# Score products of a fused attention and expert kernel: all in fp32 without split operands, half-chunk loads, two score banks, expert weights in buffers of their own

## The chip, the cores and the metric

The kernel runs on one core of a Trainium2 chip. The metric is the device time of one execution in microseconds (us). The engines are named as the profile names them: PE (TensorE, matrix products; PEld is its weight load), DVE (VectorE), ACT (ScalarE), POOL (GpSimd), SP (SyncE, which here only issues loads). All data are fp32 in memory. The inputs are random.

## The reference

The program has two halves, one feeding the other. With B = 4, N = 5056, C = 256:

```python
qn = q / (norm(q, axis=1) + 1e-6); kn = k / (norm(k, axis=1) + 1e-6)
a  = softmax(kn.transpose(0, 2, 1) @ qn / tau)      # [B, 256, 256]
x  = (v @ a).reshape(20224, 256)
skip = x @ w_skip > 0                               # only these rows go on
e  = argmax(x @ w_gate); g = 1 / sum(exp(logits - max))
x[skip] += g * (relu(x @ w1[e]) @ w2[e])            # 8 experts, 256 -> 1024 -> 256
```

So the scores are a sum over all 5056 tokens of a batch, the norms too (sums of squares over the tokens), and a batch's softmax can begin only when all of its tokens have been added. After it each token's row of `v` is multiplied by a 256 x 256 matrix, its expert is looked up, and the rows of one expert are gathered and put through two products.

## The kernel before

**Chunks.** The tokens are padded to 16 chunks (4 of each batch) of 1280 = 128 x 10. A chunk of q and of k is a tile of [128, 10, 256], which holds 10 slices j of 128 tokens each. Three kinds of work share PE:

- A: scores of a chunk, 10 steps of one slice (`scores`, lines 667-683). A step is two products, one for each half of the 256 rows of the score matrix, added up in PSUM.
- B: `v @ a` of a chunk, 5 steps of two slices (`attend`, lines 746-761), each of 12 products of fp32r halves. The matrix `a` and `v` are split into a rounded part H and a rest L (H@H + L@H + H@L).
- H: the first 7 tiles of 512 rows of the expert half, done ahead (`first_ahead`, `second_ahead`) among the last chunks of B: four steps of the first product and two of the second. They work on the tokens of the first 8 chunks.

After these come the loop over full tiles of the expert half (`Large.loop`) and one over small tiles (`Small.loop`).

**How a score step is computed.** Of the 10 slices of a chunk, slices 3 to 9 go to PE in plain fp32 (line 682, which the profile shows as two passes a product). Slices 0 to 2 are split first: ACT copies q and k to fp32r (line 622), POOL or DVE subtracts that from the original (line 625), and PE multiplies `ks_H` by the pair (`qs_H`, `qs_L`), 512 columns (line 679), and `ks_L` by `qs_H`, 256 columns (line 680). In a chunk the plain slices come first. The sums stand in two PSUM banks, one for each half of the rows, with one buffer for both (`ps_s`, bufs=1). The softmax of a batch begins by copying both to SBUF and adding their two column halves (lines 689 and 694).

**Other work on q and k.** ACT squares each half chunk (line 646), DVE adds the squares up (line 650) and folds them at the end of a batch (lines 655-657), and PE adds over partitions (lines 662-664, the tile `n`).

**Loads.** q and k are loaded by SP into three buffers of a chunk each (1280 KB apiece; the first four chunks in parts), `v` into three buffers of a half chunk. POOL writes each routed token's number and gate into the lists of the experts by 10 indirect scatters a chunk (line 839), and it gathers and scatters the rows of the expert half.

**Expert weights.** `w1r` and `w2r` hold the raw weights of the expert whose rows are done ahead. They lie in a pool that is opened where the A tiles were, so that their gathers (line 223) come after the last A step. They are split by ACT and DVE (lines 311 and 313).

**Order.** A planner (`Plan`) sets the order of all of this at build time. Each task has an engine, a cost in us, the tasks that it waits for and, for PE, a nominal time that comes from the string `ORDER`; the planner runs a list schedule with these costs and emits the instructions engine by engine in that order. On the chip each engine then takes its instructions strictly in that order, and waits where one isn't ready. So wrong costs don't make a wrong result, but an order in which an engine waits for something late while other work stands ready behind it.

Of the kernel before, what the change touches and what calls it, by code (L numbers as in the profile page):

```python
# [145 lines left out]
def attn_moe(ctx: ExitStack, tc: tile.TileContext, q, k, vt, tau, w_skip, w_gate, w1, w2, out):  # L146
# [430 lines left out]
    ps_s = in_a.enter_context(tc.tile_pool(name="ps_s", bufs=1, space=PSUM))  # L577
# [21 lines left out]
    qk, spl, vs, sums, norms, augs, lg, xos, pxs = {}, {}, {}, {}, {}, {}, {}, {}, {}  # L599
# [4 lines left out]
    def load_qk(c, j0, j1):  # L604
        b, ch = divmod(c, NCH)
        if c not in qk:
            qk[c] = [pa.tile([P, J, C], F32, name=n, bufs=3) for n in ("qt", "kt")]
        js = slice(j0, j1)
        for t, src in zip(qk[c], (q, k)):
            nc.sync.dma_start(t[:, js, :], src[b, ch * P * J : (ch + 1) * P * J, :].rearrange("(p j) c -> p j c", j=J)[:, js, :])  # L610
# [6 lines left out]

    def split_qk(c, n, part, engine=None):
        t = qk[c][n][:, :JS, :]
        if part == 0:  # L620
            spl.setdefault(c, [None, None])[n] = pa.tile([P, JS, 2, C], F32R, name=("qs", "ks")[n], bufs=1)
            S.copy(spl[c][n][:, :, 0, :], t)  # L622
        else:
            s = spl[c][n]
            {"V": V, "G": G}[engine].tensor_tensor(s[:, :, 1, :], t, s[:, :, 0, :], ALU.subtract)  # L625
# [13 lines left out]
    def squares(c, n, h):  # L639

        hs = slice(h * JH, (h + 1) * JH)
# [4 lines left out]
        S.activation(to, qk[c][n][:, hs, :], AF.Square)  # L646
# [19 lines left out]
    def scores(c):  # L666

        b, ch = divmod(c, NCH)
        if ch == 0:
            sums[b] = ps_s.tile([P, 2, 512], F32, name="s")  # L670
        qt, kt = qk[c]
        for n, j in enumerate([*range(JS, J), *range(JS)]):
            first, last = ch == 0 and n == 0, ch == NCH - 1 and n == J - 1
            for cb in range(2):
                o = sums[b][:, cb, :]
                cs = slice(cb * P, (cb + 1) * P)
                if j < JS:
                    qs, ks = spl[c]
                    T.matmul(o, ks[:, j, 0, cs], qs[:, j, :, :], start=first, stop=False, skip_group_check=True)
                    T.matmul(o[:, :C], ks[:, j, 1, cs], qs[:, j, 0, :], start=False, stop=last, skip_group_check=True)  # L680
                else:
                    T.matmul(o[:, :C], kt[:, j, cs], qt[:, j, :], start=first, stop=last, skip_group_check=True)  # L682
            yield

    def softmax(b):


        u2 = pb.tile([P, 2, 512], F32, name="u2")
        S.copy(u2, sums[b])
        u = u2[:, :, :C]  # L690
# [3 lines left out]
        V.tensor_tensor(u, u, u2[:, :, C:], ALU.add)  # L694
# [11 lines left out]
        a = u2[:, :, C:]  # L706
# [210 lines left out]
    for seg in ORDER.split():  # L917
# [19 lines left out]
    for c in range(NC):  # L937
        b, ch = divmod(c, NCH)
        ld = {}
        users = []  # L940
        for j0, j1 in PARTS.get(c, [(0, J)]):
            t = then("qk", add("D", 0.73 * (j1 - j0), lambda c=c, j0=j0, j1=j1: load_qk(c, j0, j1), due=1e9 if c else -99, hold=("part", 99) if ld else ("qk", 3)))
            t.users = [] if ld else users
            ld.update((j, t) for j in range(j0, j1))
        sp = [None, None]
        for n in range(2):
            sq = []
            for h in range(2):
                begins = ch == 0 and h == 0
                s0 = then(("sq", n), add("S", 1.18, lambda c=c, n=n, h=h: squares(c, n, h), [ld[j] for j in range(h * JH, (h + 1) * JH)], hold=None if begins else ("sqh", 3)))  # L950
                sq.append(s0)
# [9 lines left out]
            s0 = then(("sp", n), add("S", 0.75, lambda c=c, n=n: split_qk(c, n, 0), [ld[JS - 1], last_a]))  # L961
            t = sp[n] = add(*(("VG", (0.88, 1.8)) if n else ("G", 1.8)), None, [s0])
            t.f = lambda c=c, n=n, t=t: split_qk(c, n, 1, t.engine)
            users += [s0, t, *sq]
        g = scores(c)
        for j in range(J):
            deps = [ld[(j + JS) % J]] + (sp if j >= J - JS else [])
# [4 lines left out]
        users.append(t)  # L972
        if ch == NCH - 1:
            g = softmax(b)
            s0, = chain(g, ("S", 0.9), deps=[t])
            n0, = chain(g, ("T", 0.8), deps=[s0, summed[0], summed[1]])
            s = chain(g, ("V", 0.97), ("S", 1.65), ("V", 2.1), ("V", 1.45), ("S", 2.35), ("V", 0.75), deps=[n0])
# [232 lines left out]
```

## Time and profile before

| | |
|---|---|
| time, median of 3 runs | 863.21 us (861.93 to 866.31) |
| profiled execution | 867.48 us, span 864.8 us, mean granted clock of PE 0.968 |
| PE busy | 797.2 us, 92% of the span |
| DVE, ACT, POOL busy | 561.9 (65%), 394.0 (46%), 488.4 us (56%) |
| A steps on PE | from 6.3 to 251.8 us |
| B steps | from 71.9 to 439.7 us |
| first H step | at 275.68 us |
| loop over full tiles | first product at 496.6 us, last at about 775 us |
| HBM traffic | 115.98 MB read, 32.59 MB written |

The table's times of the stages are the first and the last start in PE's timeline. A row of the waits view names who waited, for whom, and then the total in us, the number of waits and the longest. In a row of windows the figures are the window, its length, the busy us (and instructions) of each engine in the order PE, PEld, DVE, ACT, POOL, the granted clock of PE as a share of full speed, the DMA engines' busy share and GB/s. In a timeline the figures are the start and the duration in us; what stands in brackets is the idle time of the engine before it and what ended it. PE's durations are modelled for their ends, so that the time of a step on PE is taken here from start to start.

### The profile page before, as it was taken

What the parts mean: (1) busy time and instruction counts of PE and PEld (TensorE: products, weight loads), DVE (VectorE), ACT (ScalarE), POOL (GpSimd) and SP (SyncE); (2) the same over time, 40 slices, a digit from 0 to 9 for tenths busy, and PEclk for the clock granted to TensorE, in tenths of its full rate; (3) what the DMA queues carried; (4) which work ended last, traced back from release to release, by engine and by line L of the source; (5) the groups of instructions that cost most, each with busy time, mean ns of one, the idle gap of its engine ahead of it and who ended that gap; (6) DMA issues with size and microseconds to landing.
All of it is one profiled execution on the core that took longest, in us unless ns stands there. A gap on an engine that the chain in (4) does not pass through costs nothing. (4 is left out here: it accounts for less than half of the span.)

```text
span 864.8 us, 13631 instructions
## 1 busy us (share of the span) xinstructions
PE 797.2 (92%) x4506; PEld 700.0 (81%) x4506; DVE 561.9 (65%) x1071; ACT 394.0 (46%) x615; POOL 488.4 (56%) x490
## 2 busy tenths in 40 slices
PE   6998999789885999999998799999999999998977
PEld 5887988678775899888887688888888888877876
DVE  3979788699985864563556755556564646556464
ACT  5769568477664443432331233333342424235444
POOL 5235378788875777567527563434334343436666
PEclk9999899898997999999999999999999999999999
DMA  8978678885527451521230241111111111106670
GB/s 319 419 280 307 238 281 261 299 320 195 184 88 267 138 164 39 184 92 38 92 83 26 73 169 49 43 49 49 49 43 48 37 48 44 49 12 240 225 296 10
DMA packets 55483, 126.36 MB, mean 146 GB/s; under 512 B 17269, under 2 KB 37517, under 8 KB 49809
## 3 DMA queue, kind: packets, MB, share of 16 engines
q1 hardware_dynamic: 14688, 62.99, 20.0%
q0 software_dynamic: 19520, 42.12, 14.7%
q10 hardware_dynamic: 21232, 20.72, 7.4%
q8 instruction: 22, 0.36, 0.2%
q14 instruction: 21, 0.16, 0.1%
HBM read 115.98 MB, written 32.59 MB: 172 GB/s over the span
## 5 line engine op out<-in xcount | busy, mean ns | idle before, releaser
L839 POOL DMA_INDIRECT lst<-pay,r_posi x160 | 184.2, 1151 | 80.5 <-issue 43.3
L216 POOL DMA_INDIRECT out<-xg,lc x78 | 80.6, 1034 | 129.8 <-DVE xg L347 113.0
L340 PE MATMUL po<-w2s,hH 128*128 128x512 f32 x384 | 136.4, 398 | 0.3 <-issue 0.3
L323 ACT ACTIVATE hH<-ph 128x512 fp32r<-128x512 f32 x96 | 57.5, 599 | 126.4 <-PE ph L320 126.4
L682 PE MATMUL s<-qt,kt 128*128 128x256 f32 x448 | 106.7, 386 | 7.9 <-DMA kt<-in_k 6.8
L341 PE MATMUL po<-w2s,hL 128*128 128x256 f32 x384 | 107.2, 279 | 0.0
L324 DVE SCALAR_TENSOR_TENSOR hL<-ph,hH 128x512 fp32r<-128x512 f32 x96 | 66.4, 692 | 54.7 <-ACT hH L323 53.3
L757 PE MATMUL px<-aH,vH 128*128 128x266 f32 x320 | 99.6, 311 | 1.3 <-ACT xo L764 1.3
L211 POOL DMA_INDIRECT xg<-out,lc x80 | 82.1, 1026 | 29.3 <-issue 18.0
L682 PEld LDWEIGHTS s<-qt,kt 128*128 128x128 f32 x448 | 83.0, 192 | 18.9 <-DMA qt<-in_q 6.3
L758 PE MATMUL px<-aL,vH 128*128 128x266 f32 x320 | 94.0, 294 | 0.0
L759 PE MATMUL px<-aH,vL 128*128 128x266 f32 x320 | 93.5, 292 | 0.0
L340 PEld LDWEIGHTS po<-w2s,hH 128*128 128x128 f32 x384 | 72.1, 188 | 17.2 <-issue 0.7
L764 ACT COPY xo<-px 128x532 f32<-128x532 f32 x80 | 47.7, 602 | 68.3 <-PE px L759 68.2
L340 PE MATMUL px<-w2s,hH 128*128 128x512 f32 x224 | 78.3, 393 | 0.0
L318 PE MATMUL ph<-xH,w1H 128*128 128x512 f32 x192 | 75.9, 395 | 2.0 <-DVE xL L288 2.0
L625 POOL TENSOR_TENSOR qs<-qt,qs 128x768 fp32r<-128x768 f32 x16 | 44.8, 2801 | 57.3 <-ACT qs L622 57.1
L319 PE MATMUL ph<-xL,w1H 128*128 128x512 f32 x192 | 75.6, 394 | 0.0
L320 PE MATMUL ph<-xH,w1L 128*128 128x512 f32 x192 | 75.6, 394 | 0.0
L341 PEld LDWEIGHTS po<-w2s,hL 128*128 128x128 f32 x384 | 72.3, 188 | 0.4
L286 ACT CAST xH<-pt 128x512 fp32r<-128x512 f32 x40 | 22.4, 591 | 101.0 <-PE pt L284 101.0
L757 PEld LDWEIGHTS px<-aH,vH 128*128 128x128 f32 x320 | 62.7, 196 | 3.3 <-ACT xo L764 2.0
(216 smaller groups left out, 1860.0 us busy)
## 6 DMA issues: line engine op xcount, KB each, us to landing
vf<-in_vt SPq DMA_DIRECT2D x32, 640.0 KB, 5.2
qt<-in_q SPq DMA_DIRECT2D x12, 1280.0 KB, 7.2
kt<-in_k SPq DMA_DIRECT2D x12, 1280.0 KB, 9.9
out<-xo ACTq DMA_DIRECT2D x12, 1280.0 KB, 9.1
qt<-in_q SPq DMA_DIRECT2D x7, 384.0 KB, 8.5
kt<-in_k SPq DMA_DIRECT2D x7, 384.0 KB, 8.3
lst<-pay,r_posi POOLq DMA_INDIRECT x160, 3.2
out<-xo ACTq DMA_DIRECT2D x4, 640.0 KB, 9.6
```

The source lines that it names most:

```text
L211: apart(G.indirect_dma_start(out=to, out_offset=None, in_=out[0:n, :], in_offset=IndirectOffsetOnAxis(ap=ls[:, 0:1], axis=0), bounds_check ...
L216: i = (G.indirect_dma_start(out=out, out_offset=IndirectOffsetOnAxis(ap=ls[:, 0:1], axis=0), in_=src, in_offset=None, bounds_check=NTOK - ...
L318: T.matmul(ph, self.w1H[:, fs], self.xH[:, kb, :], start=(kb == 0), stop=False)
L319: T.matmul(ph, self.w1H[:, fs], self.xL[:, kb, :], start=False, stop=False)
L320: T.matmul(ph, self.w1L[:, fs], self.xH[:, kb, :], start=False, stop=(kb == 1))
L340: T.matmul(po, self.hH[:, f, ts], self.w2s[:, f, :, :], start=(f == 0), stop=False, skip_group_check=True)
L341: T.matmul(po[:, :C], self.hL[:, f, ts], self.w2s[:, f, 0, :], start=False, stop=(f == NFB - 1), skip_group_check=True)
L682: T.matmul(o[:, :C], kt[:, j, cs], qt[:, j, :], start=first, stop=last, skip_group_check=True)
L757: T.matmul(px[:, i, :NA], vH[:, kb, js], aH[:, kb, :], start=(kb == 0), stop=False)
L758: T.matmul(px[:, i, :NA], vH[:, kb, js], aL[:, kb, :], start=False, stop=False)
L759: T.matmul(px[:, i, :NA], vL[:, kb, js], aH[:, kb, :], start=False, stop=(kb == 1))
L839: i = G.indirect_dma_start(out=lst, out_offset=IndirectOffsetOnAxis(ap=posi[:, t : t + 1], axis=0), in_=pay[:, t0 + t, :], in_offset=None, ...
```

## The change

It does these things together:

- All 10 slices of a chunk go to PE in plain fp32. The splits of q and k on ACT, POOL and DVE and the tiles `qs` and `ks` are gone.
- The sums of a batch take one bank (2 x 256 columns) instead of two, and there are two of them, so that a batch's first step waits for the softmax copy of the batch before the last one.
- The addition of the two column halves in the softmax is gone; the exponentials get a tile of their own.
- q and k are loaded by half chunks (640 KB each) into five buffers of a half chunk, where there were three of a whole one. A buffer is free when the squares of that half and its fifth step are done. The first half of chunk 0 is loaded in two parts.
- `w1r` and `w2r` get buffers of their own. Their gathers then wait only for the choice of the expert (`look`), and stand in POOL's order behind the scatters of chunk 7. The splits of the weights still go to tiles where A's tiles were, and so wait for the last A step.
- The costs that the planner uses are changed: a step of A 0.865 (0.86 and 0.65 before), of B 1.475 (1.34), of H 2.74 and 5.62 (2.56 and 5.15), a pair of scatters 2.6 (2.09) and some smaller ones, so that the order on every engine is another one. `ORDER` itself is the same.

```diff
-JS = 3
-
-PARTS = {0: [(3, 5), (5, J), (0, 3)], 1: [(3, 6), (6, J), (0, 3)], 2: [(3, 6), (6, J), (0, 3)], 3: [(3, 6), (6, J), (0, 3)]}
+NQ = 5
...
             self.xg = [rows([P, 4, C], F32, name=f"xg{h}") for h in range(3)]
+            self.w1r = rows([P, 2 * F], F32, name="w1r")
+            self.w2r = rows([P, NFB * C], F32, name="w2r")
...
         def weights(self):
             wp = ctx.enter_context(tc.tile_pool(name="wl", bufs=1, reuse_waits="tile"))
-            self.w1r = wp.tile([P, 2 * F], F32, name="w1r")
-            self.w2r = wp.tile([P, NFB * C], F32, name="w2r")
...
-    ps_s = in_a.enter_context(tc.tile_pool(name="ps_s", bufs=1, space=PSUM))
+    ps_s = in_a.enter_context(tc.tile_pool(name="ps_s", bufs=2, space=PSUM))
...
-    def load_qk(c, j0, j1):
+    def load_qk(c, h, j0, j1):
         b, ch = divmod(c, NCH)
-        if c not in qk:
-            qk[c] = [pa.tile([P, J, C], F32, name=n, bufs=3) for n in ("qt", "kt")]
+        if (c, h) not in qk:
+            qk[c, h] = [pa.tile([P, JH, C], F32, name=n, bufs=NQ) for n in ("qt", "kt")]
...
-    def split_qk(c, n, part, engine=None):
-        t = qk[c][n][:, :JS, :]
-        if part == 0:
-            spl.setdefault(c, [None, None])[n] = pa.tile([P, JS, 2, C], F32R, name=("qs", "ks")[n], bufs=1)
-            S.copy(spl[c][n][:, :, 0, :], t)
-        else:
-            s = spl[c][n]
-            {"V": V, "G": G}[engine].tensor_tensor(s[:, :, 1, :], t, s[:, :, 0, :], ALU.subtract)
...
-            sums[b] = ps_s.tile([P, 2, 512], F32, name="s")
-        qt, kt = qk[c]
-        for n, j in enumerate([*range(JS, J), *range(JS)]):
-            first, last = ch == 0 and n == 0, ch == NCH - 1 and n == J - 1
+            sums[b] = ps_s.tile([P, 2, C], F32, name="s")
+        for j in range(J):
+            qt, kt = qk[c, j // JH]
             for cb in range(2):
...
-                if j < JS:
-                    qs, ks = spl[c]
-                    T.matmul(o, ks[:, j, 0, cs], qs[:, j, :, :], start=first, stop=False, skip_group_check=True)
-                    T.matmul(o[:, :C], ks[:, j, 1, cs], qs[:, j, 0, :], start=False, stop=last, skip_group_check=True)
-                else:
-                    T.matmul(o[:, :C], kt[:, j, cs], qt[:, j, :], start=first, stop=last, skip_group_check=True)
+                T.matmul(sums[b][:, cb, :], kt[:, j % JH, cb * P : (cb + 1) * P], qt[:, j % JH, :], start=(ch == 0 and j == 0 and cb == 0), stop=(ch == NCH - 1 and j == J - 1), skip_group_check=True)
...
-        V.tensor_tensor(u, u, u2[:, :, C:], ALU.add)
...
-                    now += (0.88 if i < J - JS else 0.66) if x == "A" else 1.36 if x == "B" else 2.6 if i < 4 else 5.2
+                    now += 0.87 if x == "A" else 1.48 if x == "B" else 2.75 if i < 4 else 5.65
...
-            if j == 0 and ch == 0 and b:
-                deps.append(freed_s[b - 1])
-            t = then("A", add("T", 0.86 if j < J - JS else 0.65, lambda g=g: next(g), deps, nominal["A", c, j]))
+            if j == 0 and ch == 0 and b > 1:
+                deps.append(freed_s[b - 2])
+            t = then("A", add("T", 0.865, lambda g=g: next(g), deps, nominal["A", c, j]))
...
-            t = then("B", add("T", 1.34, None, [sv[j > 2][1], sv[j >= 2][1], ready_a[b]], nominal["B", d, j], hold=("px", 2, 1)))
+            t = then("B", add("T", 1.475, None, [sv[j > 2][1], sv[j >= 2][1], ready_a[b]], nominal["B", d, j], hold=("px", 2, 1)))
...
-        in_order["sc"] = chain(g, *[("G", 2.09)] * (J // 2), deps=[routed[d], in_order.get("sc")], due=nominal["B", d, 4] + 15)[-1]
+        in_order["sc"] = chain(g, *[("G", 2.6)] * (J // 2), deps=[routed[d], in_order.get("sc")], due=nominal["B", d, 4] + 15)[-1]
...
-    wg1 = add("G", 1.05, scores_done, [look, norms_read, last_a])
-    wg2 = add("G", 1.05, lambda: gather_w(w2, large.w2r, large.wd), [wg1])
-    wd1 = add("D", 2.9, None, [wg1])
-    wd2 = add("D", 2.9, None, [wg2])
+    wr1 = add("G", 1.3, lambda: gather_w(w1, large.w1r, large.wc), [look])
+    wr2 = add("G", 1.3, lambda: gather_w(w2, large.w2r, large.wd), [wr1])
+    wd1 = add("D", 2.9, None, [wr1])
+    wd2 = add("D", 2.9, None, [wr2])
+    wg1 = wg2 = add("S", 0.05, scores_done, [wr2, norms_read, last_a])
```

The sequence of the scheduled instructions shows what this moves. The first place is PE's first steps. Before:

```order
L682 MATMUL s<-qt,kt 128x256 x14
L679 MATMUL s<-qs,ks 128x512
L680 MATMUL s<-qs,ks 128x256
L679 MATMUL s<-qs,ks 128x512
L680 MATMUL s<-qs,ks 128x256
```

Now:

```order
L662 MATMUL s<-qt,kt 128x256 x110
L649 MATMUL n<-sqq,ones 128x256
L651 MATMUL n<-ones,sqk 128x2 x2
L662 MATMUL s<-qt,kt 128x256 x26
L703 MATMUL m<-ident,aug 128x128 x4
```

The products that read `qs` and `ks` are gone, and with them the places at which PE waits for the splits; the norms of batch 0 stand behind 55 steps, where they stood behind 53.

The second place is POOL between the last scatters of chunk 7 (`lst<-pay`) and the first gathers of rows (`xg<-out`), for which `lN` holds the list. Before:

```order
L228 TENSOR_LOAD ad_2347
L228 ISA x2
L229 ISA
L229 DMA lN<-lst 128x56
L625 TENSOR_TENSOR ks<-kt,ks 128x3x256
L389 COPY lc_151<-lN 128x8
L211 DMA xg_145<-out,lc_151 128x256 x4
L389 COPY lc_149<-lN 128x8
L211 DMA xg_143<-out,lc_149 128x256 x4
L223 DMA w1r<-in_w,wc 128x2048
L223 DMA w2r<-in_w,wd 128x2048
```

Now:

```order
L817 DMA lst<-pay,r_posi 168960x2 x80
L221 DMA w1r<-in_w,wc 128x2048
L221 DMA w2r<-in_w,wd 128x2048
L226 TENSOR_LOAD ad_2113
L226 ISA x2
L227 ISA
L227 DMA lN<-lst 128x56
L387 COPY lc_153<-lN 128x8
L209 DMA xg_145<-out,lc_153 128x256 x4
```

The 11 splits that stood among these scatters and behind them are gone (one of them, of `ks`, is among the rows of before), and the two gathers of raw weights have moved from behind eight gathers of rows to ahead of the list.

The third place is PE near the end of the work ahead: the count of chunk 15's tokens (`m<-r_rc`), on which the last scatters and all later lists wait. Before it stood between the two products of the sixth tile:

```order
L320 MATMUL px<-xH,w1L 128x512
L814 MATMUL m<-r_rc,tri_r 128x8
L815 MATMUL m<-r_rc,ones_r 128x8
L284 MATMUL pt<-ident,xg_145 128x128 x4
L340 MATMUL px<-w2s,hH 128x512
```

Now it stands in the middle of that tile's second product, one of its two steps later:

```order
L339 MATMUL px<-w2s,hL 128x256
L792 MATMUL m<-r_rc,tri_r 128x8
L793 MATMUL m<-r_rc,ones_r 128x8
L338 MATMUL px<-w2s,hH 128x512
```

More of the change, by code (lines that the diff above doesn't have):

```diff
@@ L597, in end_lists @@
         yield
-    qk, spl, vs, sums, norms, augs, lg, xos, pxs = {}, {}, {}, {}, {}, {}, {}, {}, {}
+    qk, vs, sums, norms, augs, lg, xos, pxs = ({} for _ in range(8))
     sqs = [pa.tile([P, JH, C], F32, name=f"sq{n}", bufs=1) for n in "qk"]
     sqh = {}
-    def load_qk(c, j0, j1):
+    def load_qk(c, h, j0, j1):
         b, ch = divmod(c, NCH)
-        if c not in qk:
-            qk[c] = [pa.tile([P, J, C], F32, name=n, bufs=3) for n in ("qt", "kt")]
-        js = slice(j0, j1)
-        for t, src in zip(qk[c], (q, k)):
-            nc.sync.dma_start(t[:, js, :], src[b, ch * P * J : (ch + 1) * P * J, :].rearrange("(p j) c -> p j c", j=J)[:, js, :])
+        if (c, h) not in qk:
+            qk[c, h] = [pa.tile([P, JH, C], F32, name=n, bufs=NQ) for n in ("qt", "kt")]
+        for t, src in zip(qk[c, h], (q, k)):
+            nc.sync.dma_start(t[:, j0:j1, :], src[b, ch * P * J : (ch + 1) * P * J, :].rearrange("(p j) c -> p j c", j=J)[:, h * JH + j0 : h * JH + j1, :])
     def load_v(n):
@@ L639, in squares @@
     def squares(c, n, h):
-        hs = slice(h * JH, (h + 1) * JH)
         if c % NCH == 0 and h == 0:
@@ L705, in softmax @@
         yield
-        a = u2[:, :, C:]
+        a = pb.tile([P, 2, C], F32, name="a")
         mx = pb.tile([P, 2], F32, name="mx")
@@ L938, in attn_moe @@
         b, ch = divmod(c, NCH)
[L939 to L945, printed above, removed]
+        ld, users = {}, ([], [])
+        for h in range(2):
+            for j0, j1 in [(0, 2), (2, JH)] if c == 0 and h == 0 else [(0, JH)]:
+                t = then("qk", add("D", 0.76 * (j1 - j0), lambda c=c, h=h, j0=j0, j1=j1: load_qk(c, h, j0, j1), due=1e9 if c else -99, hold=("part", 99) if j0 else ("qk", NQ)))
+                t.users = [] if j0 else users[h]
+                ld.update((h * JH + j, t) for j in range(j0, j1))
         for n in range(2):
-            sq = []
             for h in range(2):
@@ L960, in attn_moe @@
                 summed[n] = add("V", 1.53, lambda n=n: fold_squares(n), [summed[n]])
[L961 to L964, printed above, removed]
         g = scores(c)
         for j in range(J):
-            deps = [ld[(j + JS) % J]] + (sp if j >= J - JS else [])
-            if j == 0 and ch == 0 and b:
-                deps.append(freed_s[b - 1])
-            t = then("A", add("T", 0.86 if j < J - JS else 0.65, lambda g=g: next(g), deps, nominal["A", c, j]))
+            deps = [ld[j]]
+            if j == 0 and ch == 0 and b > 1:
+                deps.append(freed_s[b - 2])
+            t = then("A", add("T", 0.865, lambda g=g: next(g), deps, nominal["A", c, j]))
+            if j % JH == JH - 1:
+                users[j // JH].append(t)
         last_a = t
-        users.append(t)
         if ch == NCH - 1:
             g = softmax(b)
-            s0, = chain(g, ("S", 0.9), deps=[t])
+            s0, = chain(g, ("S", 0.5), deps=[t])
             n0, = chain(g, ("T", 0.8), deps=[s0, summed[0], summed[1]])
-            s = chain(g, ("V", 0.97), ("S", 1.65), ("V", 2.1), ("V", 1.45), ("S", 2.35), ("V", 0.75), deps=[n0])
+            s = chain(g, ("V", 0.42), ("S", 1.65), ("V", 2.2), ("V", 1.85), ("S", 2.35), ("V", 0.75), deps=[n0])
             m0, = chain(g, ("T", 0.45), deps=s[-1:])
@@ L1000, in attn_moe @@
         for h in range(2):
-            ld = then("v", add("D", 1.85, lambda d=d, h=h: load_v(2 * d + h), hold=("vf", 3)))
+            ld = then("v", add("D", 1.88, lambda d=d, h=h: load_v(2 * d + h), hold=("vf", 3)))
             s0 = then("vH", add("S", 1.18, lambda d=d, h=h: split_v(d, h, 0), [ld], hold=("vH", 3)))
@@ L1089, in attn_moe @@
             g = large.first_ahead(2 * i)
-            t = then("H", add("T", 2.56, None, tr + w1s[1::2], nominal["H", x, i], hold=("px", 2, 1)))
+            t = then("H", add("T", 2.74, None, tr + w1s[1::2], nominal["H", x, i], hold=("px", 2, 1)))
             t.f = lambda g=g, t=t: product(g, t)
@@ L1099, in attn_moe @@
             g = large.second_ahead(x, 2 * i)
-            t = then("H", add("T", 5.15, None, [v for n in range(4) for v in in_order["hL", n]] + w2s[1::2], nominal["H", x, 4 + i], hold=("px", 2, 1)))
+            t = then("H", add("T", 5.62, None, [v for n in range(4) for v in in_order["hL", n]] + w2s[1::2], nominal["H", x, 4 + i], hold=("px", 2, 1)))
             t.f = lambda g=g, t=t: product(g, t)
```

14 lines of the change are left out of this document (5 added, 9 removed).

## The prediction

> **What bounds the kernel now.** I read the windows by stage first: A alone to 66 us, A and B to 276, then B and H. Later instructions are the same in both kernels.
>
> ```profile
> core 0: us, PE busy (x) PEld busy (x) DVE busy (x) ACT busy (x) POOL busy (x), PEclk, DMA share, GB/s
> 0.00:66.00 66.00, 58.14 (x274) 49.98 (x274) 46.61 (x47) 42.52 (x45) 24.16 (x43) 1.00 0.87 340
> 66.00:100.00 34.00, 30.13 (x170) 26.82 (x170) 28.40 (x40) 26.28 (x31) 13.84 (x2) 0.90 0.77 287
> 100.00:276.00 176.00, 148.29 (x910) 135.75 (x909) 146.43 (x263) 113.36 (x152) 139.63 (x109) 0.92 0.68 236
> 276.00:494.00 218.00, 210.07 (x1201) 184.29 (x1201) 132.96 (x348) 75.72 (x139) 136.78 (x138) 0.98 0.30 92
> ```
>
> PE is the fullest engine everywhere, so the time is PE's work, plus what PE waits, plus what it loses at a lower clock. In the first and the last stage there is little to win: 58.1 of 66 us busy with the first load in front, and 210 of 218. The loss is in the middle: 31.6 us idle (3.9 + 27.7) and a clock of 0.90 and 0.92. DVE (174.8 of 210 us) and POOL (153.5, without the pause behind each scatter) are close behind PE there, so that each of the three can be late for the others.
>
> Next, the waits of PE up to 300 us:
>
> ```profile
> PE s L679 <- POOL qs L625: 12.6, 3, 6.3
> PE px L318 <- ACT w1H L311: 7.7, 1, 7.7
> PE s L682 <- DMA kt<-in_k: 6.8, 2, 6.3
> PE n L662 <- DVE sqq L657: 4.4, 2, 2.2
> PE n L664 <- DVE sqk L657: 1.6, 2, 0.8
> PE s L680 <- POOL ks L625: 1.5, 2, 1.1
> PE s L682 <- ACT u L689: 1.1, 1, 1.1
> PE s L680 <- DVE ks L625: 0.2, 1, 0.2
> ```
>
> A third of the idle time is for the splits, and a quarter for the expert weights before the first H step. Of the waits for loads 6.3 us are the start, and later loads of q and k make PE wait 0.5 us in all. The places, from PE's timeline:
>
> ```profile
> 86.16 0.80 PE L679 MATMUL s<-qs,ks 128*128 128x512 f32 x1 [3.38 <-POOL qs L625]
> 159.67 0.80 PE L679 MATMUL s<-qs,ks 128*128 128x512 f32 x1 [6.32 <-POOL qs L625]
> 230.50 0.50 PE L679 MATMUL s<-qs,ks 128*128 128x512 f32 x1 [2.88 <-POOL qs L625]
> 275.68 0.79 PE L318 MATMUL px<-xH,w1H 128*128 128x512 f32 x1 [7.73 <-ACT w1H L311]
> ```
>
> The reader is to see that products take 0.80 us behind such a wait that take 0.40 elsewhere. The windows of 5 us show it as the granted clock:
>
> ```profile
> 85.00:90.00 5.00, 3.84 (x14) 0.50 0.99 395
> 160.00:165.00 5.00, 5.00 (x19) 0.65 1.00 371
> 195.00:200.00 5.00, 3.91 (x12) 0.50 0.49 168
> 230.00:235.00 5.00, 4.50 (x21) 0.68 0.19 56
> 255.00:260.00 5.00, 4.27 (x19) 0.57 0.53 155
> 275.00:280.00 5.00, 3.20 (x7) 0.50 0.68 271
> 280.00:285.00 5.00, 5.00 (x18) 0.70 0.40 132
> ```
>
> What each loses is its busy time by what the clock lacks of 1: 1.9, 1.8, 2.0, 1.4, 1.8, 1.6 and 1.5 us. So a wait costs itself and about 2 us behind it.
>
> Why are the splits late? Rows of POOL's and DVE's timelines:
>
> ```profile
> 74.13 11.97 POOL L625 TENSOR_TENSOR qs<-qt,qs 128x768 fp32r<-128x768 f32 x1 [9.84 <-ACT qs L622]
> 84.63 2.83 DVE L650 TENSOR_TENSOR sqk<-sqk,sqh 128x1280 f32<-128x1280 f32 x1 [0.19 <-ACT sqh L646]
> 245.08 6.16 DVE L650 TENSOR_TENSOR sqq<-sqq,sqh 128x1280 f32<-128x1280 f32 x1 [1.58 <-ACT sqh L646]
> 245.65 1.83 POOL L625 TENSOR_TENSOR qs<-qt,qs 128x768 fp32r<-128x768 f32 x1
> ```
>
> A split on POOL took 11.97 us while DVE went from one sum of two operands to the next, and 1.83 elsewhere; in turn sums of DVE took 2.83 and 6.16 us beside a split. They hold each other up, and PE waits for the one or the other. The two later waits have the split behind scatters in POOL's queue.
>
> **The change part by part.** *Waits removed.* The three rows for splits (12.6 + 1.5 + 0.2 = 14.3 us) have no instruction left to wait for: fp32 steps read what was loaded, in the cases above long before (the split that read it started 12 us ahead). The weights (7.7): their gather is issued here.
>
> ```profile
> 265.68 0.99 POOL L223 DMA_INDIRECT w1r<-in_w,wc  x1 [0.30 <-issue]
> ```
>
> PE's row at 275.68 is 10 us behind it. Now the gather stands ahead of the list and is hidden by the remaining A and B steps; what stays is the four casts and subtractions behind the last A step, which four B steps cover. If that cover is gone, some 3 us return. The copy of the sums (1.1): the other bank takes the next batch. Together 23.1 us, with the clock behind these waits (85, 160, 230, 275 and 280 us): 1.9 + 1.8 + 1.4 + 1.6 + 1.5 = 8.2.
>
> The Trainium skill, "TensorE: Matmul & The Clock Gate", Part 1, has the clock halve only after idle gaps of some 3.4 us, for one more window of that length. By it two of the four gaps would count, at 1.7 us each, 3.4 in place of 8.2, and the sum below would be 4.8 less, 845 us. The trace disagrees for the shorter gaps: 0.50 behind 3.38 us and 0.68 behind 2.88.
>
> *DVE relieved.* Its waits for the norms (4.4 + 1.6) and the clock behind them (the rows at 195 and 255: 2.0 + 1.8) come to 9.8 us. DVE loses its splits, the final addition, and the delays beside POOL: 1.4 and 4.7 us in the two rows above, against 1.48 for an undisturbed sum. But DVE remains 83% busy and the order is new. Bounds: all 9.8 and nothing; I take half, 4.9.
>
> The skill's page "SBUF — State Buffer", "Who interferes with whom", makes the two engines' port an exclusive lock in which the loser waits for one instruction. By it a split would be late by 1.5 us, not by 10; here the trace goes further. The same section has sums of two operands spare the writing of scatter descriptors, so nothing is taken for faster scatters.
>
> *Work added.* PE's timeline gives the price of a step:
>
> ```profile
> 14.70 0.58 PE L679 MATMUL s<-qs,ks 128*128 128x512 f32 x1
> 30.97 0.58 PE L679 MATMUL s<-qs,ks 128*128 128x512 f32 x1
> 23.71 0.40 PE L679 MATMUL s<-qs,ks 128*128 128x512 f32 x1
> 24.42 0.40 PE L679 MATMUL s<-qs,ks 128*128 128x512 f32 x1
> ```
>
> Two chunks lie between the first two rows, so that one takes 8.135 us; a split step takes 0.71 (the last two rows). A plain one is then (8.135 - 3 x 0.71) / 7 = 0.858, a chunk of ten 8.58, and sixteen chunks cost 16 x 0.445 = 7.1 us more. All of it is on PE, so on the path wherever PE doesn't wait.
>
> *Moved and new waits.* On POOL the two gathers of weights now stand ahead of the first list: at 0.99 + 0.30 each (row at 265.68) the rows of the first H step come 2.6 us later. Bounds: 0, if PE is later than POOL, and 2.6; I take 2.6. The half loads double SP's issues; with five halves a half has two chunks of steps to land. New waits of that kind weren't there and have no row: bounds 0 and 4, twice what two such rows of 0.5 to 1 us cost with their clock; I take 2.
>
> At the end of the work ahead the count of chunk 15 is one step later on PE.
>
> ```profile
> 450.55 0.17 PE L814 MATMUL m<-r_rc,tri_r 128*128 128x8 f32 x1
> 462.29 0.60 PE L284 MATMUL pt<-ident,xg 128*128 128x128 f32 x4
> 455.31 0.98 POOL L839 DMA_INDIRECT lst<-pay,r_posi  x1 [15.30 <-DVE r_posi L836]
> 480.18 1.00 POOL L211 DMA_INDIRECT xg<-out,lc  x1 [0.30 <-issue]
> ```
>
> From the count to the last gather of the loop's rows POOL needs 30.6 us (480.18 + 1.0 - 450.55), and they land some 2 later. PE has had 38 us of work for it until the loop's first transposes, and has 5.8 less now (half of 450.55 to 462.29). That is even; I take 1, and 0 to 4 as bounds.
>
> *Sum.* 23.1 + 8.2 + 4.9 - 7.1 - 2.6 - 2 - 1 = 23.5 us off. From the profiled 867.48 that is 844.0; that execution lay 4.3 over the median of the runs, 863.21, which becomes 839.7. I say **840 us**. With all terms at their bad ends (0 of the 9.8, and 2.6, 4 and 4 of new waits) it is 24.2 - 10.6 = 14 less, with all at the good ones 34: 829 to 850.
>
> **The rivals.**
>
> *More is won.* All of DVE's 9.8 goes and the new waits don't come: 23.1 + 8.2 + 9.8 - 7.1 = 34 us, 829. For it: DVE loses the 6.1 us of the two delayed sums, its splits besides, and is free for a sixth of the stage today. Against it: PE's stage shrinks too, and the order is a planner's.
>
> *The waits move.* DVE and B's operands are late where the splits were, and half of the 31.3 us of waits and clock returns: 23.5 - 15.7 = 8, 855 us. For it: DVE at 83% with PE at 85. Against it: B's own waits are 0.6 to 1.1 us today.
>
> *The weights aren't what the first H step waits for.* Its rows come from chunk 7's scatters over ten POOL instructions; if they take the weights' place, 7.7 + 3.1 return: 13 us are left, 850. For it: POOL's queue was full to 245 us. Against it: eleven of its splits of about 2 us are gone.
>
> *Slower: the smaller ring starves PE.* Five halves hold 2.5 chunks where three were held, and SP takes loads in order, so that one load of v that waits for a buffer holds q and k up. Loads are long:
>
> ```profile
> kt<-in_k SPq DMA_DIRECT2D x12, 1280.0 KB, 9.9
> ```
>
> Of 93 steps after 66 us about 19 halves are read. If each came late by more than 23.5 / 19 = 1.2 us, the gain would be gone; at 2 us the time is 878. For it: a DMA share of 0.99 and 1.00 at 85 and 160 us. Against it: 0.5 us of waits today, at 236 GB/s on average and up to 395.
>
> **How the numbers follow.** The forecast gets 0.45, more 0.20, the moved waits 0.15, the rows in place of the weights 0.12, the starved ring 0.08. The range of 822 to 856 leaves out the ring, and little of the others. Half a per cent, 4.3 us, is what a measurement can tell from none. Faster holds all of the forecast, of more and of the rows, and 0.13 of the moved waits: 0.90. The rest of those and 0.01 of the ring make 0.03 for the same, and 0.07 are slower.
>
> **What would show it.** In the profile after, the product `s` waits for nothing but loads and the bank; chunks of A take 8.6 us; DVE's sums take 1.48 throughout; the first H step comes near 253 us, and the clock to 276 us is above 0.95. Wrong would be: waits of `s` for q or k of some us each (the ring), the rows `xg` ending a long wait at the first H step, or PE as idle as before for DVE or ACT.

## The result and the profile after

The change made the kernel faster. Its runs have a median of 838.28 us (836.43 to 841.51, four runs) against 863.62 us of the kernel before beside them (861.93 to 866.31, four runs): the ratio is 0.9708, with a 95% interval of 0.9669 to 0.9747. That is 25.3 us less, where 23.5 were forecast; 838 lies 2 us from the predicted 840. The profiled execution took 838.44 us, its span is 836.7 us (864.8 before) and PE's mean granted clock 0.989 (0.968). One kernel below had three of its ten runs in a slower state of the chip; its median and ratio leave them out.

The windows by stage, of the changed kernel, with the first H step near 250 us and the loop near 467:

```profile
core 0: us, PE busy (x) PEld busy (x) DVE busy (x) ACT busy (x) POOL busy (x), PEclk, DMA share, GB/s
0.00:66.00 66.00, 58.87 (x266) 51.16 (x266) 33.71 (x42) 32.92 (x32) 7.18 (x36) 1.00 0.85 325
66.00:100.00 34.00, 32.68 (x200) 30.12 (x201) 30.65 (x45) 25.26 (x29) 3.29 (x3) 1.00 0.99 374
100.00:253.00 153.00, 144.27 (x901) 132.32 (x900) 121.39 (x274) 103.82 (x143) 108.46 (x95) 0.98 0.76 259
253.00:470.00 217.00, 207.77 (x1200) 182.25 (x1199) 126.89 (x323) 73.17 (x133) 141.39 (x144) 0.99 0.34 100
```

The middle stage, A with B, ended 23 us sooner (253 in place of 276), PE is idle there for 10.0 us in place of 31.6 (1.3 and 8.7), and the clock went from 0.90 and 0.92 to 1.00 and 0.98. The last stage shown is nearly the same as before. So all that was won lies ahead of the first H step and just behind it. The first H product starts at 248.81 us (275.68 before), the loop at 466.6 (496.6), the small tiles at 747.0 (776.6). A window that ends just at the first H step gives the balance, first before, then after:

```profile
0.00:275.68 275.68, 236.24 (x1350) 212.23 (x1350) 221.15 (x346) 181.84 (x226) 177.63 (x154) 0.94 0.74 267
```

```profile
0.00:248.81 248.81, 231.63 (x1353) 210.31 (x1353) 182.09 (x346) 159.55 (x199) 115.66 (x130) 0.99 0.82 297
```

PE's idle time fell from 39.4 to 17.2 us, by 22.3, and its busy time by 4.6, though A is more work: the clock gave back more than that work took. Together that is the 26.9 us by which the step comes sooner. The other 3 us up to the loop lie just behind the step, before and after:

```profile
276.00:290.00 14.00, 12.88 (x45) 9.78 (x45) 11.95 (x27) 8.45 (x16) 8.29 (x8) 0.75 0.32 114
```

```profile
249.00:263.00 14.00, 14.00 (x62) 11.63 (x63) 13.14 (x27) 6.63 (x13) 10.95 (x11) 0.90 0.32 94
```

These 14 us held 12.88 us of work at 0.75 before (1.1 idle and 3.2 lost to the clock) and 14.00 at 0.90 after (1.4 lost), which makes 2.9.

What PE still waits for up to 260 us:

```profile
PE s L662 <- DMA kt<-in_k: 7.7, 2, 6.5
PE pt L282 <- DMA xg<-out,lc: 4.4, 1, 4.4
PE m L792 <- DVE r_rc L789: 2.1, 3, 0.9
PE m L711 <- ACT aT L706: 1.6, 2, 1.3
PE pt L282 <- DVE xL L286: 1.4, 1, 1.4
```

The product `s` waits for loads alone, 6.5 us of it at the start, and no row of the norms is left. But at the first H step the weights have a successor, the rows `xg` and their transposes. PE's timeline has the place:

```profile
240.37 0.30 PE L282 MATMUL pt<-ident,xg 128*128 128x128 f32 x1
245.03 1.18 PE L282 MATMUL pt<-ident,xg 128*128 128x128 f32 x3 [4.36 <-DMA xg<-out,lc]
247.61 1.12 PE L282 MATMUL pt<-ident,xg 128*128 128x128 f32 x4 [1.40 <-DVE xL L286]
248.81 0.77 PE L316 MATMUL px<-xH,w1H 128*128 128x512 f32 x1
```

Up to 300 us only this wait has a lower granted clock behind it. The first two of these windows of 5 us lay behind a wait for splits before, the last two are those at the wait:

```profile
85.00:90.00 5.00, 5.00 (x30) 4.57 (x29) 3.61 (x6) 3.71 (x5) 0.00 (x0) 1.00 1.02 421
160.00:165.00 5.00, 5.00 (x35) 4.74 (x34) 4.54 (x4) 4.54 (x6) 4.09 (x4) 1.00 1.03 410
245.00:250.00 5.00, 3.57 (x12) 2.71 (x13) 2.77 (x6) 3.74 (x7) 3.78 (x5) 0.51 0.13 32
250.00:255.00 5.00, 5.00 (x20) 3.92 (x19) 4.63 (x14) 2.37 (x4) 4.09 (x4) 0.81 0.02 1
```

That is 3.57 x 0.49 + 5 x 0.19 = 2.7 us lost behind 4.36 us of idle time and the 1.40 that follow. By the Trainium skill, "TensorE: Matmul & The Clock Gate", Part 1, one window of some 3.4 us at half the clock would lose 1.7, an estimate from its figures. It agrees that such a gap drops the clock; the loss here is larger, and whether the second gap is the reason no run here shows.

The groups of instructions have the score steps (640 passes of PE, four for each of 160 steps) and DVE's sums:

```profile
L662 PE MATMUL s<-qt,kt 128*128 128x256 f32 x640 | 149.2, 384 | 7.7 <-DMA kt<-in_k 7.7
L637 DVE TENSOR_TENSOR sqq<-sqq,sqh x28: 1481/1486/1494, 13.0 to 219.6; 128x1280 f32<-128x1280 f32 x28
L637 DVE TENSOR_TENSOR sqk<-sqk,sqh x28: 1482/1486/1493, 14.4 to 221.1; 128x1280 f32<-128x1280 f32 x28
```

The last two rows give the shortest, the median and the longest of 28 sums: none is over 1.49 us, where 6.16 stood before.

### The profile page after: what moved, and what is told of

Same layout as the page of the kernel before. It is cut to its first block, busy times and chain, and to the rows that moved or that the text cites. A ratio compares the mean times of both kernels' runs of the same rounds, so it can differ in the third digit from the quotient of the medians.

```text
span 836.7 us, 13561 instructions
## 1 busy us (share of the span) xinstructions
PE 790.2 (94%) x4506; PEld 695.8 (83%) x4506; DVE 519.4 (62%) x1055; ACT 369.8 (44%) x583; POOL 430.5 (51%) x470
## 5 line engine op out<-in xcount | busy, mean ns | idle before, releaser
L817 POOL DMA_INDIRECT lst<-pay,r_posi x160 | 177.0, 1106 | 164.4 <-DVE r_posi L814 93.1
L662 PE MATMUL s<-qt,kt 128*128 128x256 f32 x640 | 149.2, 384 | 7.7 <-DMA kt<-in_k 7.7
L662 PEld LDWEIGHTS s<-qt,kt 128*128 128x128 f32 x640 | 119.0, 192 | 22.7 <-issue 8.1
L209 POOL DMA_INDIRECT xg<-out,lc x80 | 83.5, 1044 | 31.6 <-issue 19.5
L737 PE MATMUL px<-aH,vL 128*128 128x266 f32 x320 | 91.8, 287 | 0.0
L736 PE MATMUL px<-aL,vH 128*128 128x266 f32 x320 | 91.3, 285 | 0.0
L344 DVE SCALAR_TENSOR_TENSOR xg<-po,lc,xg 128x256 f32<-128x256 f32 x48 | 23.2, 484 | 63.8 <-PE po L339 53.1
L339 PE MATMUL px<-w2s,hL 128*128 128x256 f32 x224 | 62.7, 280 | 0.0
L735 PEld LDWEIGHTS px<-aH,vH 128*128 128x128 f32 x320 | 60.4, 189 | 1.9 <-ACT xo L742 0.5
```

Source lines behind the costliest of these rows:

```text
L209: apart(G.indirect_dma_start(out=to, out_offset=None, in_=out[0:n, :], in_offset=IndirectOffsetOnAxis(ap=ls[:, 0:1], axis=0), bounds_check ...
L339: T.matmul(po[:, :C], self.hL[:, f, ts], self.w2s[:, f, 0, :], start=False, stop=(f == NFB - 1), skip_group_check=True)
L662: T.matmul(sums[b][:, cb, :], kt[:, j % JH, cb * P : (cb + 1) * P], qt[:, j % JH, :], start=(ch == 0 and j == 0 and cb == 0), stop=(ch == ...
L735: T.matmul(px[:, i, :NA], vH[:, kb, js], aH[:, kb, :], start=(kb == 0), stop=False)
L736: T.matmul(px[:, i, :NA], vH[:, kb, js], aL[:, kb, :], start=False, stop=False)
L737: T.matmul(px[:, i, :NA], vL[:, kb, js], aH[:, kb, :], start=False, stop=(kb == 1))
```

## The experiments

The theory: the gain is waits that are gone (splits, weights, the copy of the sums) and the clock behind them, and a part of DVE's delays. The rivals were that the new costs and the order that follows from them bring it, that one part alone brings it, that DVE is worth more than was taken, and that the smaller ring costs. Several chips were used. On one chip (the costs alone, and the first runs of the splits on DVE, the plain products and the late weights) the kernel before took 906.68 us, on another (the second runs of these three, and the whole-chunk buffers) 901.36, so that only ratios to it compare with other chips; what is different there is told at the end. Neither the change itself nor a trace of the kernel before was taken on those two. The other four runs were made on a third chip, where the kernel before took 865.76 us.

**The costs alone.** The kernel before, with the planner's main new costs (0.715 for a step with a split; those of H too, not shown) and nothing else:

```diff
-            t = then("A", add("T", 0.86 if j < J - JS else 0.65, ...
+            t = then("A", add("T", 0.865 if j < J - JS else 0.715, ...
...
-            t = then("B", add("T", 1.34, ...
+            t = then("B", add("T", 1.475, ...
...
-        in_order["sc"] = chain(g, *[("G", 2.09)] * (J // 2), ...
+        in_order["sc"] = chain(g, *[("G", 2.6)] * (J // 2), ...
```

> The kernel before with the planner's costs alone changed to those of the change (a step of A 0.865 or 0.715 with a split, B 1.475, H 2.74 and 5.62, a pair of scatters 2.6); splits and all else stay. Theory: the splits still collide with DVE's sums and stand in POOL's queue, so that PE's waits for them stay above 8 us and the time is within 8 us of before, 856 to 868. Rival (the order is what mattered): 840 to 848, with the waits for splits gone.

Measured: 898.57 us, ratio 0.9891 (0.9831 to 0.9951), 8 us off. A wait for splits of about the size of before stands:

```profile
PE s L679 <- POOL qs L625: 9.8, 2, 9.2
```

So a new order of the old work wins about 1%, with the splits' waits still there; it doesn't do what the change did.

**The old costs in the changed kernel**, on the third chip, beside the change itself run again:

```diff
-            t = then("A", add("T", 0.865, ...
+            t = then("A", add("T", 0.86 if j < 7 else 0.65, ...
...
-            t = then("B", add("T", 1.475, ...
+            t = then("B", add("T", 1.34, ...
...
-        in_order["sc"] = chain(g, *[("G", 2.6)] * (J // 2), ...
+        in_order["sc"] = chain(g, *[("G", 2.09)] * (J // 2), ...
```

> The changed kernel itself, beside the others of this group on their chip. Expected by every theory: its ratio to the kernel before is 0.965 to 0.976 as when first timed; if this chip runs the kernel before more slowly, the ratio is what the other kernels of this group are compared with.

> The changed kernel with the old costs of A (0.86 and 0.65), B, H and scatters, so that the order is made for a faster PE and POOL than there is; all else as changed. Theory (the splits, the weights and DVE's relief are the gain, the costs add little): 0 to 6 us over the changed kernel. Rival (the order is a large part): 12 us or more over the changed kernel, with waits of PE between A and B steps.

Measured: the change 837.68 us, ratio 0.9693 (0.9653 to 0.9733), with the first H step at 248.8 us again; with the old costs 835.63, ratio 0.9665 (0.9618 to 0.9712). The intervals overlap: within the change the new costs bring nothing that can be told.

**The splits on DVE.** The kernel before, with all splits of q and k on DVE, none on POOL:

```diff
-            t = sp[n] = add(*(("VG", (0.88, 1.8)) if n else ("G", 1.8)), None, [s0])
+            t = sp[n] = add("V", 0.88, None, [s0])
```

> The kernel before with all subtractions of the splits on DVE instead of POOL. Theory (POOL's queue and its collision with DVE make the splits late): PE's waits for splits fall from 14 to under 6 us, no sum of DVE takes over 1.6 us, scatters end earlier; DVE has some 17 us more work, so that a part is given back: 850 to 858 us. Rival (it is DVE's fill that makes everything late, and POOL's part is harmless): DVE above 90% in the stage up to the first H step, waits for norms grow, 866 us or more.

> The same kernel as splits_on_dve (the kernel before with the subtractions on DVE). idle_splits has shown DVE held up by each split on POOL. Theory: without them there DVE's sums are never held up, PE's waits for splits fall under 3 us, and the time is 8 to 14 us under the kernel before, ratio 0.984 to 0.991. Rival (DVE is full, what POOL does is harmless): ratio 1.00 or more.

Measured: 895.35 us, ratio 0.9879 (0.9819 to 0.9939), and 889.95, ratio 0.9856 (0.98 to 0.9912): 11.3 and 11.4 us off. PE waits for a split for 0.3 us at most, and no sum on DVE takes over 1.5 us. What stays, here from the first run, are the waits that the change removed in other ways:

```profile
PE px L318 <- ACT w1H L311: 9.1, 1, 9.1
PE n L662 <- DVE sqq L657: 3.5, 2, 1.8
PE n L664 <- DVE sqk L657: 1.6, 2, 0.8
```

So the place of the splits, and not only their work, is worth 1.2 to 1.4%, where the change brought 3 on other chips.

**Plain fp32 products alone.** The kernel before with no slice split, but whole-chunk loads, one buffer for the sums, late weights and old costs:

```diff
-JS = 3
+JS = 0
...
-        S.copy(u2, sums[b])
+        S.copy(u2[:, :, :C], sums[b][:, :, :C])
...
-        V.tensor_tensor(u, u, u2[:, :, C:], ALU.add)
```

> The kernel before with the score steps alone changed: all ten slices in plain fp32, no splits and no final addition, q and k loaded by whole chunks (the first four in two or three parts), one buffer for the sums, weights late, the old costs. Theory (the splits' waits, the clock behind them and DVE's relief are the larger part): 14.3 us of waits, 4.7 of clock and 4.9 of DVE less, 7.1 of work more, so about 17 us under the kernel before, 846 us; PE's wait for the cast of the weights stays at 7 to 8 us. Rival (the new costs and with them the order do it): within 5 us of before, since the order is made with the old costs. Rival (the smaller loads and the second bank do it): within 5 us of before too.

> The same kernel as fp32_alone (the kernel before with all score steps in plain fp32 and nothing else of the change), since the first group ran on a chip on which the kernel before took 907 us and engines stood idle for tens of us behind no wait that the profile shows. Theory: 15 to 20 us under the kernel before, ratio 0.977 to 0.983, with 7 us of wait for the weights left. Rival (most of the gain is elsewhere): ratio above 0.990, as the first group gave.

Measured: 899.79 us, ratio 0.9912 (0.987 to 0.9954), and 895.13, ratio 0.9907 (0.9847 to 0.9966), so 6 to 8 us off where the theory wanted about 17. The trace of the second has the wait for the weights still, at half its size; that of the first has none:

```profile
PE px L318 <- ACT w1H L311: 3.9, 1, 3.9
```

The splits' waits are gone here as well. Ahead of the first H step the theory fares better than in the total: the step comes at 259.7 and 265.4 us, where the kernel before had it at 275.68 on its chip, though PE has 36 and 37 more products ahead of it (three steps of B). If that compares across chips, part of what was won there is lost again behind it; why isn't settled (see what stays open, below).

**The changed kernel with late weights.** The raw weights lie again where A's tiles were and are gathered behind the last A step:

```diff
-            self.w1r = rows([P, 2 * F], F32, name="w1r")
-            self.w2r = rows([P, NFB * C], F32, name="w2r")
...
+            self.w1r = wp.tile([P, 2 * F], F32, name="w1r")
+            self.w2r = wp.tile([P, NFB * C], F32, name="w2r")
...
-    wr1 = add("G", 1.3, lambda: gather_w(w1, large.w1r, large.wc), [look])
+    wg1 = add("G", 1.05, scores_done, [look, norms_read, last_a])
```

> The changed kernel with the raw weights back in the pool that opens after the last A step, and their gathers behind it. Theory (the weights' own buffers were worth 7.7 us and the clock, less the 2.6 us that their gathers put ahead of the list): the first H step waits 6 to 8 us for the cast of the weights, and the time is 4 to 8 us above the changed kernel, 842 to 846 us. Rival (the rows are what the first H step waits for, the weights are hidden anyway): no difference beyond 2 us, 837 to 840.

> The same kernel as weights_late (the changed kernel with the weights' gathers behind the last A step). Theory: 4 to 8 us over the changed kernel's 0.970, so a ratio of 0.975 to 0.980, with 6 to 8 us of wait for the cast of the weights. Rival (the rows hide it): 0.969 to 0.972, since the request for the list also comes earlier, which list_first has shown to be worth 4.7 us.

Measured: 882.13 us, ratio 0.9721 (0.9672 to 0.9771), and 882.73, ratio 0.9768 (0.969 to 0.9847). Both intervals overlap the change's; the first ratio lies at the rival's range and the second in the theory's, so that the times decide nothing. In neither trace does the first H step, at 266.0 and 264.7 us, wait for the weights: POOL gathers them at 251.75 us in the first.

```profile
236.11 0.59 POOL L227 DMA_DIRECT2D lN<-lst  x1 [1.39 <-DMA lst<-pay,r_posi]
238.20 0.74 POOL L387 COPY lc<-lN 128x8 int32<-128x8 int32 x1 [1.50 <-DMA lN<-lst]
251.75 0.99 POOL L221 DMA_INDIRECT w1r<-in_w,wc  x1 [2.29 <-DMA vf<-in_vt]
```

So here the weights needn't be gathered before the list to be in time: they come 14 us ahead of the step, and the kernel before needed 10 from the gather to the step that waited for them. The planner has put 36 products more (three steps of B) ahead of the first H step in these kernels, which helps to cover them. From the last A step to the first H step it is 17.2 us, as in the change (248.8 to 266.0, and 231.5 to 248.8). What buffers of their own bought on a chip like that of the change isn't shown. These rows also show what the list's read takes when no weights are ahead of it, 2.1 us from its start to the copy behind it.

**The list before the weights.** The changed kernel, but POOL reads the list first and gathers the weights behind it:

```diff
-    lst0 = add("D", 0.16, None, [add("G", 1.05, lambda: next(rows), [look, listed0, stored[D0 - 1]])])
+    asked = add("G", 1.05, lambda: next(rows), [look, listed0, stored[D0 - 1]])
+    lst0 = add("D", 0.16, None, [asked])
...
-    wr1 = add("G", 1.3, lambda: gather_w(w1, large.w1r, large.wc), [look])
+    wr1 = add("G", 1.3, lambda: gather_w(w1, large.w1r, large.wc), [asked])
```

> The changed kernel with the request for the first list ahead of the two gathers of raw weights on POOL, so that they run while the list is on its way. Theory (the gathers ahead of the list hold up the first H step's rows by 2.6 us): PE's wait for the rows at the first H step falls from 4.4 us to about 2, and the time by 2 to 4 us, ratio to the changed kernel 0.995 to 0.998. Rival (the rows wait for the last scatters and the landing of chunk 7 in memory, not for POOL's queue): no change.

Measured: 832.96 us (832.15 to 833.64), ratio 0.9632 (0.9595 to 0.9669), which is 4.7 us less than the change beside it and a little more than was expected; all four runs lie below all four of the change. It beats both kernels. POOL's timeline in the change, and then here:

```profile
222.29 1.19 POOL L221 DMA_INDIRECT w1r<-in_w,wc  x1 [0.31 <-issue]
223.79 1.15 POOL L221 DMA_INDIRECT w2r<-in_w,wd  x1 [0.31 <-DVE sqq L643]
224.94 0.61 POOL L227 DMA_DIRECT2D lN<-lst  x1
236.22 0.19 POOL L387 COPY lc<-lN 128x8 int32<-128x8 int32 x1 [10.67 <-DMA lN<-lst]
237.31 1.07 POOL L209 DMA_INDIRECT xg<-out,lc  x1 [0.90 <-POOL lc L387]
```

```profile
226.93 0.60 POOL L227 DMA_DIRECT2D lN<-lst  x1 [2.44 <-DMA lst<-pay,r_posi]
227.83 1.19 POOL L221 DMA_INDIRECT w1r<-in_w,wc  x1 [0.30 <-DVE sqk L643]
229.32 1.03 POOL L221 DMA_INDIRECT w2r<-in_w,wd  x1 [0.31 <-issue]
230.79 0.81 POOL L387 COPY lc<-lN 128x8 int32<-128x8 int32 x1 [0.44 <-DMA lN<-lst]
231.87 1.03 POOL L209 DMA_INDIRECT xg<-out,lc  x1 [0.27 <-POOL lc L387]
```

A small read, issued behind two gathers of 1 MB each, took 11.3 us until POOL could go on (224.94 to 236.22); issued 2 us later but ahead of them, 3.9. The DMA packets of the two traces say why: all three transfers go through one queue. In the change its 256 packets of 8 KB, the two gathers, start from 227.7 us on, and the list's 16 packets of 1792 bytes start behind them, at 235.0; with the list first they start at 230.0 and the gathers' at 230.3. The first gather of rows starts 5.4 us sooner, the wait for `xg` is gone, and what PE waits for at this place is 0.9 us:

```profile
PE pt L282 <- DVE xL L286: 0.5, 1, 0.5
PE px L317 <- DVE xL L286: 0.4, 1, 0.4
```

**Idle splits.** The changed kernel, with 20 subtractions of 768 columns on POOL, as many as it had of splits before. Nothing reads what they write:

```diff
+    def idle_split(c, n):
+        o = pa.tile([P, 3, C], F32, name="idle", bufs=1)
+        t = qk[c, 0][n][:, :3, :]
+        G.tensor_tensor(o, t, qk[c, 0][1 - n][:, :3, :], ALU.subtract)
...
+        for n in range(2 if ch == NCH - 1 else 1):
+            t = add("G", 1.8, lambda c=c, n=n: idle_split(c, n), [ld[0], last_a])
+            users[0].append(t)
```

> The changed kernel with 20 extra subtractions on POOL, one or two a chunk, of the size of the old splits, from the loaded q and k into a tile that nothing reads. PE waits for none of them; they only stand in POOL's queue, hold their half of q and k until done, and meet DVE's sums. Theory (half of the old splits' harm was on POOL and DVE, not in PE's direct wait): DVE's sums show delays of 1.5 us and more again, the scatters end later, and the time is 4 to 10 us over the changed kernel. Rival (only PE's direct waits counted): within 2 us.

Measured: 853.51 us (851.45 to 856.28), ratio 0.9869 (0.9823 to 0.9914): 15.8 us more than the change beside it, and more than was expected. DVE's timeline and POOL's at one place:

```profile
71.08 3.11 DVE L642 TENSOR_TENSOR sqq<-sqq,sqh 128x1280 f32<-128x1280 f32 x1
74.20 3.02 DVE L642 TENSOR_TENSOR sqk<-sqk,sqh 128x1280 f32<-128x1280 f32 x1
77.77 1.48 DVE L629 TENSOR_TENSOR vL<-vf,vH 128x1280 fp32r<-128x1280 f32 x1
79.17 3.13 DVE L642 TENSOR_TENSOR sqq<-sqq,sqh 128x1280 f32<-128x1280 f32 x1
```

```profile
70.09 2.75 POOL L618 TENSOR_TENSOR idle<-qt,kt 128x768 f32<-128x768 f32 x1 [18.59 <-DMA kt<-in_k]
72.92 2.96 POOL L618 TENSOR_TENSOR idle<-kt,qt 128x768 f32<-128x768 f32 x1
78.19 2.75 POOL L618 TENSOR_TENSOR idle<-qt,kt 128x768 f32<-128x768 f32 x1 [2.32 <-DMA kt<-in_k]
```

A sum that meets a subtraction takes up to 1.65 us more, and a subtraction up to 1.15 us more than the shortest (1.81). The window up to the first H step, to be laid beside the change's of 248.81 us, and the waits that came with it:

```profile
0.00:264.10 264.10, 236.12 (x1352) 213.78 (x1353) 212.04 (x346) 159.80 (x199) 162.37 (x151) 0.98 0.79 279
```

```profile
PE m L797 <- DVE r_rc L794: 9.0, 6, 2.4
PE px L741 <- DVE aL L724: 2.3, 1, 2.3
PE m L708 <- DVE aug L703: 2.3, 1, 2.3
```

DVE executes the same 346 instructions and is busy for 212.0 us in place of 182.1. Of the 30 us, 14 are the 56 sums, and most of the rest small operations of the routing, of which several take twice as long. PE waits 13.6 us for DVE in these three rows, where the change has 2.1 for `r_rc` alone, and for no split, since none is read. So the splits' cost reaches PE through DVE as well as through their results. One reservation: the planner made a new order with them, and they also stand in POOL's queue (the last scatter of chunk 7 ends at 237.9 us, 222.1 in the change) and hold the halves of q and k.

**Late weights and whole-chunk buffers.** The kernel with late weights, and three buffers of a whole chunk in place of five halves, still loaded by halves:

```diff
-        if (c, h) not in qk:
-            qk[c, h] = [pa.tile([P, JH, C], F32, name=n, bufs=NQ) for n in ("qt", "kt")]
+        if (c, 0) not in qk:
+            ts = [pa.tile([P, J, C], F32, name=n, bufs=3) for n in ("qt", "kt")]
+            for i in range(2):
+                qk[c, i] = [t[:, i * JH : (i + 1) * JH, :] for t in ts]
```

> As weights_late_2, and q and k in three buffers of a whole chunk again (still loaded by halves, but a buffer is free only when both halves are used). With early weights this doesn't fit in memory, so it is compared with weights_late_2. Theory (the ring's size and grain are hidden): within 2 us of weights_late_2. Rival (the finer ring lets loads come earlier and spreads the DMA): 4 us or more over it, with waits of the steps for q or k.

Measured: 894.63 us, ratio 0.9906 (0.985 to 0.9963), 12 us more than late weights alone on the same chip, and the intervals don't overlap, if barely. The time is as the rival had it, but its sign is missing: PE's waits for loads of q and k are 6.8 us, and 7.7 with the halves. The first H step is 2 us later (266.7 and 264.7), so that most of the 12 us lie behind it, when all of q and k has been used. That the five halves are better than three chunks is thus not shown. Whole-chunk buffers with early weights weren't tried.

## Why the prediction was right

The total was right, by 2 us, and so was the mechanism of most terms. Some sizes were off, in opposite directions, so that part of the agreement is luck. Another part is that of the executions: between the two profiled ones, from which the terms are taken, the gain is 29.0 us, 5.5 more than the sum. By its own steps:

- *Waits removed (23.1).* Right in the rows: 14.3 us for splits, 7.7 for the weights and 1.1 for the copy of the sums have none left. But whether the reason given for the weights, that the early gather hides them, was needed is open: with late weights, and three more steps of B ahead of it, the first H step doesn't wait for them either. (Their share of the idle time, put at a quarter, was a fifth, 7.7 of 39.4 us; the sum doesn't use it.)
- *The clock behind them (8.2).* About right, by two errors. By windows of 5 us, as the prediction counts, PE lost 12.0 us to the clock up to the first H step before, and 1.2 after; of the 10.8, 3.8 are the norms', so that 7.0 are left where 5.1 were counted. The prediction took one window of 5 us behind each wait, and the next could still be low (0.82 from 90 to 95 us). The other 3.1 were counted at and behind the first H step, and there the new wait for rows kept 1.4 of 3.2 us. The gaps that are left between the start and 240 us are of 1.3 us and less, with a clock of 1.00. By the rule of the Trainium skill, "TensorE: Matmul & The Clock Gate", Part 1, as the prediction took it, the estimate was 845 us; the runs lie 7 below, which alone doesn't test the rule, since other terms were off too.
- *DVE relieved (4.9, half of 9.8).* Mis-sized. The waits for the norms went entirely, 6.0 us, and the clock behind them too, since up to 245 us every window of 5 us is at 1.00 now; the rival "more is won" had this right. The term was also too narrow. It counted only two delays of sums, of 1.4 and 4.7 us, and only waits for norms. With idle splits the change loses 15.8 us, and DVE is busy 30 us longer: small operations of the routing suffer as the sums do, and PE waits for their results. How much of the 15.8 us is POOL's longer queue and the halves held isn't separated.
- *Work added (7.1).* Right, a little low. PE starts a pass every 0.216 us (the median of the starts in the timeline) and a step has four, so that a chunk takes 8.64 us where 8.58 were forecast, and 16 chunks 8.1 us more than before.
- *The weights ahead of the list (2.6).* Mis-sized, and this is the step that failed: it cost 4.7 us by the run that has the list first. It counted what POOL needs to issue two gathers, and not what their 2 MB do to the list's read behind them: 11.3 us in place of 2.1 to 3.9. The first H step waits 5.8 us for rows and their transposes, with 2.7 us of clock behind. The rival of the rows named this place, but for late scatters; the last scatter of chunk 7 ends at 222.0 us.
- *New waits (2).* About right: 1.2 us for one load where 0.5 stood, and 2.1 for `r_rc` where 0.5 stood for the same count.
- *The hand-off to the loop (1).* Nothing came of it: the stage from the first H step to the loop is 3 us shorter, by the clock at its start.
- *The ring.* Loads of q and k make PE wait 7.7 us, 6.5 of it at the start, so nothing starved.

Of the signs named ahead, the waits of `s`, the sums of 1.48 us, the chunks of 8.6 and the clock above 0.95 came true; the first H step came at 249 and not 253. The row named as wrong, `xg` ending a long wait there, came too.

**What stays open.** The parts timed alone won 6 to 8 us (the plain products), 8 (the costs) and 11 (the place of the splits). The first and the third overlap, since both take the splits off POOL, so that the parts, with that counted once, fall short of the change's 25. All these ran on the chips on which a kernel takes some 40 us more. There, mostly between the first H step and the loop, engines sit idle in a way that hardly appears in the traces from the other chips. Its rows are named `issue` or `remote`, which name no instruction of this core as the one waited for; on the other chips PE's rows named `issue` come to 4.3 us at most in this stage. With late weights:

```profile
PE px L316 <- issue: 12.2, 3, 10.1
ACT hH L399 <- remote: 16.4, 2, 10.3
```

The stage takes 247 to 271 us there and 217 to 221 elsewhere, and the loop behind it the same 280 to 284. The plain products alone have the longest, 271.3 and 259.3 us. Ahead of the first H step PE has 14.0 us of such rows in the first trace with late weights, and 2.8 in the second. Such waits can swallow or add what an edit does ahead of them, and the single-part ratios carry that. Whether the parts work only together, or these chips hide a part of it, can't be told from these runs; it would take the change and a trace of the kernel before on such a chip.

## What to carry to other kernels

An operation that one engine does on the side can be paid for by another whose instructions it holds up: before moving work to an idle POOL, look at DVE's durations beside POOL's, not at POOL's idle time. When a transfer is moved forward, count what it puts ahead of others in the same DMA queue by its bytes, not by its issue time; a small read that decides what comes next belongs ahead of large ones. And a wait of PE's of 3 us cost 5 here, since the clock behind it is part of the price.

## What the runs showed of the hardware that was not expected

DVE's busy time holds the time in which it is held up. The same 346 instructions read 182.1 us in the change and 212.0 with 20 subtractions on POOL, so that DVE's share of 83% in the stage before was partly waiting. The Trainium skill, "SBUF — State Buffer", "Who interferes with whom", has the loser wait for one instruction. The sums beside idle splits agree, with 3.02 to 3.13 us for 1.48 beside subtractions of 1.81 and more; the split of 11.97 us in the kernel before doesn't, where POOL lost to one sum of DVE after another. And the chips differ: the same kernel before took 863.62, 865.76, 901.36 and 906.68 us as medians. Traces of other kernels from the two slow chips have most of the difference in one stage, in which engines wait for nothing that the profile names.
